# Transposing batch 3's last keys, queries and u with the DMA crossbar instead of TensorE

## The chip, the cores and the metric

The kernel runs on one core of a Trainium2 chip. Its engines are TensorE (PE, with its weight loads as PEld), VectorE (DVE), ScalarE (ACT), GpSimd (POOL) and SyncE (SP), which here only issues transfers; sixteen DMA engines carry these out. The metric is the device time of one execution in microseconds (us). Before the change it is 174.1 us, the median of 3 runs (174.01 to 174.3).

## The reference

Four batches, eight heads, 768 tokens, 48 columns a head. A recurrence with a decay per key column gives x (768 tokens by 384 columns in each batch), and a mixer over tokens and then channels follows:

```
state = alpha_t * state + k_t (outer) v_t        # per batch and head, 48 x 48
x_t   = q_t . state                              # heads side by side: x is 768 x 384
h  = relu(x^T @ w_tok1) @ w_tok2                 # over tokens, 768 -> 256 -> 768
u  = x + h^T
out = u + relu(u @ w_ch1) @ w_ch2                # over channels, 384 -> 1536 -> 384
```

## The kernel before

**Tiling.** A batch is six chunks of 128 tokens; chunks are numbered through the batches, so batch 3 has 18 to 23. Inputs are float32, and all that TensorE reads is bf16. Batch 0 and parts of batch 1 take chunks in pairs (`paired_chunks`); the later ones go by `natural_run`, and only those matter here.

**A chunk.** ACT takes the logarithm of alpha (`la`). PE sums it over the tokens with a triangular matrix (`cum`, L352), ACT exponentiates with both signs (`ek`, `eq`), and GpSimd multiplies keys and queries with the results (`pkk`, `pkq`, L275), eight heads of 64 columns each, 48 of them used. `s_transpose` brings both into a layout with columns on the partitions: `row_tiles` (L289) has PE transpose 64 x 64 pieces through an identity, sixteen a chunk, into two banks, and `s_transposed` (L297) copies the two banks to `tkq` on ACT or DVE. Then PE multiplies keys with queries (`gt`, L387), DVE masks (`gm`, L309), and PE forms the output of the chunk (`y`, L423, with the state's share in `between`, L338). The state goes through `state` (PE, L411), `st` (DVE) and `ss` (GpSimd, L322); GpSimd also makes `al` and casts v (`vb`). The output is evicted as `x`.

**The mixer.** For a batch with all six x: `tok1` (L602), a relu (`ht`), `tok2` (L651), and `u`, which DVE adds into the x tiles (L657). The channel part needs u with the columns on the partitions. In batches 1 to 3 (`separate`) PE transposes three chunks at a time with `row_tiles` (`utp`, 18 pieces of 64 x 64 for each half of the batch), and ACT and DVE copy them to `ut` (L669). Batch 0 (`mixed`) computes u transposed directly. `channel` then has 24 `ch1` (L691, three matmuls of 384 columns each), their relu (`rt`, L589 and L591), and for each chunk `ch2` in three parts of four matmuls (L715), the sum `o` (L728) and the store.

**What sets the order.** One list, `ORDER`, written out in numbers. Each item is an operation of the graph in the order of its creation, with the engine (A, D, P) where there is a choice and the banks behind a point; `f` is a matmul on zeros (`fill`, L792) that keeps PE busy and computes nothing. Each engine takes its own operations in that order, and waits in it. ch1 and ch2 of one batch stand between the chunk work of the next. All transfers are issued by SP, in the same order too: 86 loads and 25 stores. The tiles of the chunks come round: four `pkk`, `pkq` and `tkq`, six `o`, twelve x, two `ut`.

Of the kernel before, what the change touches and what calls it, by code (L numbers as in the profile page):

```python
# [17 lines left out]
FUSE = 99  # L18
FETCH, BLOCK, AHEAD, ARRIVES = 193, 256, 449, (4.5, 30.0, 3.0)
# [6 lines left out]
0 1 f0 2 f0 f0 f0 f0 f0 3 f0 f0 f0 f0 f0 4 28 f0 29 f0 f0 30.0 5 31.1 32 f2 f2 38 6 f2 35 f2 33 f2 f2 f2 39 f2 34 f2  # L26
36 40 f2 43.2 41 7 f3 66 47.3 f4 65 48 44 49A 50D f4 67.4 46A 45D 68.5 69 f6 51.67 75 72 54.01 8 70 52 f3 f3 76 f3 73
f3 77 f3 80.3 78 f2 9 84.2 56 f6 85 105 81 71 f6 104 87D f6 f6 10 86A f6 f6 83D 106.6 82A 55 107.5 108 53 91.14 11 114
88.23 92 f0 42P 37A f0 f0 109 90 f0 58.07 115 89 57.13 60A 93 f2 116 12 f2 f2 59 f2 f2 f2 112 f2 111 63 61 117 14
123.2 64A f0 62 f0 124 74A 79P 119.0 110 16 120 125D 126A f4 94.41 122A 121D 18 96 127.57 97 130.36 95.20 128 113A  # L30
118P 100 132 98 102 133.4 99A 20 131 13P f5 103A 169.5 101 163.6 24 166.2 f3 15P 129 141.3 135 142.0 143 136 134.17
17P 137 139 145 138D 147 140A 144 146 259 148 150 149 151 19D 152 172.4 178.1 162A 161D 175.7 f0 173 176 174A 167 177D
260 164 168A 170 22D 21P 165A 179 f0 171A 23D f0 261 f0 180A f0 189.0 201.3 190A 195.4 262 202A 181.7 27D 25P 196A
185.2 26D 182A 153 193.6 186A 211.5 264 194D 223.1 263 212D 227.0 224A 265.3 228A 266.4 155 267 217.7 273 270 207.2
274 209.6 268 300 208D 218A 276 213.5 210D 215.1 214A 269 187.0 301 271 216A 203.4 188A 219.3 275 204A 302 225.2 220A
154D 199.7 272 226A 278.65 277 279 200A 303 221.1 280D 281A 156P 183.0 222A 282 283 184A 292.43 284D 285A 197.2 304
294 286.71 157 305 198D 289.05 205.6 287 306.4 288 206A 159 191.2 308 291 307.7 309 311 239.6 296 314 343 290 315
249.1 297 192D 293.54 344 312 319.37 298 295A 345 254.0 316 299A 234.2 158A 346 317 244.5 347 310 313 160D 240 318 348
245 351 241 349 320 352.4 242A 321D 246 322A 354 235 247D 353 350 358 236 356 243 323 362 324 237D 333.64 357 325A
326D 376.5 238 363.2 335 250 248 355 364 336 486 365 327.37 251 487 329 366 367 330.62 328 252A 488 255 332 368 256  # L40
339 369 359.73 331 257A 370.12 340 229.4 361A 360D 253 372D 371A 377 373.60 258 510 334.73 375 489 381.21 341 490 374
337 230 342A 378 382 338A 491 379.5 383 231 380A 492 384.0 232D 511.6 385A 493 513 388.3 512 516 233 386.2 389A 514
517 494 521 495 515 387D 522.7 390.1 496 523 398.5 391 524 394.4 526 396.0 399 392.6 395 400.3 527 535.2 393 518.17
401 497 402.54 528 519A 397 529.63 525 403A 553.1 404D 498 520A 536 405.05 530A 416.4 499 554 406A 440.7 407D 555 531A
500 417D 420.2 539 434.6 421D 441A 501 532.10 435A 550.53 534 422.4 502 430.2 551 546 423A 540.7 533 431A 452.6 558
552 442.0 541 537.5 453D 503 542 438.4 544 538D 559.2 439A 556.1 443D 504 560 543 412.3 545 557D 561 426.6 413D 505
432.7 564 427A 410.5 506 433A 446.4 562 411A 565 408.0 507 447A 563 572.1 577 450.2 409D 508 454.3 573 451A 547.67 574
455D 566.54 509 548A 578.0 549D 591.1 568A 567D 448.2 720 592 580 424.3 584 449D 579 588.76 583 721 425A 569.54 590
418.1 596 582 436.2 570 419A 414.0 571 437A 581 597.3 593 589 722 610.6 575.5 598 444.1 415D 599 601 723 576A 594.2
611 445A 481.4 595D 602 724 744 428.7 476.0 600 429A 725 603 604.35 612 585.61 605A 726 466.2 587D 586A 477 727 606A  # L50
482 728 607.73 751 615.16 609 483 729 755 616 471.5 608 478 617 613.3 730 479 472 614A 484 618.1 480 762 456.7 619D
473 485 773 622.6 731 474 732 620.0 623A 475 457 621A 733 458 734 634.3 459 630.4 735 628.1 635 632.5 631 624.6 780
460 626.0 629 461.7 625 792 736 627 462 737 633 463 636.34 738 464 639.16 637A 467 638D 640A 641D 465 468 799 774.0
469 745.5 775 793.7 656.4 746 778 747 756.3 470 650.6 795 739 757 749 684.1 651D 740 758 644.2 685D 776 748 662.5 794
760 645D 741 660.6 811 663D 657A 678.3 750 742 661D 787.0 769.1 679A 812.7 770 759 668.2 743 777 813 761 672.5 788 814
664.4 669A 673D 789 670.6 665A 666.3 779 671A 646.1 830 667D 682.0 798 647A 831.7 683A 806.2 781.54 797 832 807 763.63
833 752.10 765D 658.2 783A 835 754D 764A 674.7 753D 659D 782A 686.3 808 675D 800.40 687A 803.16 796 802D 816 784.25
801A 766.73 804 680.0 768 818 654.4 681A 836 767 648.1 655A 844.3 786 642.0 649A 817 771.7 785 822.41 643A 652.5 772A
805 834 837 790.2 824 815 653A 809.0 791A 823 838.76 810A 819.51 825.2 839D 820A 828.4 840D 676.0 821A 826 715.7 829D
827 677A 849.65 841.21 845 716 843 846 700.4 851 695.0 850 696 842 852.3 688.1 853D 847.5 689A 705.6 848D 697 854.2  # L60
698 699 717 855A 710.3 718 711 701 719 702 856.1 703 704 712 857A 690.5 713 858.0 714 868.2 859 862.7 860.4 869 864.1
863 866.3 691 861 867 692 865 706 693 873.02 694 870.74 874A 875D 707 871D 872A 910.3 708 894.1 911A 709 880.5 895A
908.2 881D 906.0 909A 912.7 907A 900.4 913A 876.6 901A 896.3 877A 918.1 897A 914.5 919D 904.2 915A 922.0 905D 902.7
923D 920.4 903A 898.6 921A 916.3 899A 888.1 917A 890.5 889A 884.2 891D 878.0 885A 886.7 879A 882.4 887A 892.6 883D
929.3 893A 939.1 930 931 940 932 944.5 933 945 946 934.2 947 941 948 924.0 942 925 943 926 935 927 936 928 949.7 937
950 938 951 954.4 955 952 956 953 957 958
# [12 lines left out]
class Graph:  # L79
# [5 lines left out]
    def add(self, name, costs, emit, reads=(), writes=(), prio=0, dma=None, new=(), tail=0.0, rows=False, loose=False, n=0, late=0.0):  # L85
        self.ops.append(Op(costs, emit, new))
        return self.ops[-1]
# [6 lines left out]
def kernel(  # L94
# [12 lines left out]
    nc = tc.nc  # L107
    B, H, S, D = q.shape
    C = 128
# [232 lines left out]
    def natural_front(n):  # L342
# [7 lines left out]
        def cum(e):  # L350
# [3 lines left out]
            for j in range(4):  # L354
                pe.matmul(ps[:, HD + j : HD + j + 1], lhsT=la[:, 2 * j : 2 * j + 2, :], rhs=ones_col,  # L355
                          start=True, stop=True, skip_group_check=True)
# [478 lines left out]
```

## Time and profile before

| what | value |
|---|---|
| median of 3 runs | 174.1 us |
| the profiled execution | 174.24 us |
| its span, first to last instruction | 172.5 us |
| PE busy | 166.5 us, 96% |
| DVE, ACT, POOL busy | 102.0, 96.0, 72.3 us |
| HBM read and written | 25.17 and 4.72 MB |

Times in the profile count from the start of the span. A row of the groups has the line, engine and operation, what it writes and reads, how many there are, then busy time and mean duration in nanoseconds, then idle time just before them and what ended it. The end of a matmul is modelled, and matmuls overlap, so PE's pace is better read from the chain of waits, where many of one kind stand in one stretch: 72 matmuls of 384 columns in 11.70 us. SPq is SP's own queue. Releasers are inferred.

### The profile page before, as it was taken

The page shows a single profiled execution, that of the slowest core. Times are in us where ns is not written, and L with a number is a line of the kernel's source. Part 1 is how long each engine was busy: PE and PEld are TensorE (multiplying, and loading weights), DVE is VectorE, ACT ScalarE, POOL GpSimd, SP SyncE. Part 2 cuts the span into 40 slices and gives each one's busy share as a digit, 9 for nine tenths or more (in the row PEclk, how much of TensorE's full clock was granted, in tenths as well). Part 3 has the DMA queues.
Part 4 walks back from the last instruction along what each step waited for, and adds up shares of the span by engine and source line. Part 5 has one row for each costly group of instructions (what it writes and reads, how often), then busy time and mean ns, then how long its engine had stood idle before and what let it go on. Part 6 is the DMA issues. An engine that isn't in the chain of part 4 may idle for free.

```text
span 172.5 us, 5143 instructions
## 1 busy us (share of the span) xinstructions
PE 166.5 (96%) x2099; PEld 106.8 (62%) x2099; DVE 102.0 (59%) x212; ACT 96.0 (56%) x206; POOL 72.3 (42%) x114
## 2 busy tenths in 40 slices
PE   7999979999999999999999999999999999999993
PEld 3566656665666567566666665666676656656562
DVE  3159977544653597689593727495988248132231
ACT  2577552699865655497887231699771112865000
POOL 7252542319485782944877111499941000000000
PEclk9999999999999999999999999999999999999999
DMA  5999999999998999999999999995000221100133
GB/s 134 261 261 265 232 335 398 309 234 337 256 307 168 205 254 219 225 170 198 165 204 151 196 219 223 211 210 92 4 4 0 79 104 50 46 4 0 46 115 113
DMA packets 86150, 30.20 MB, mean 175 GB/s; under 512 B 79600, under 2 KB 85104, under 8 KB 86128
## 3 DMA queue, kind: packets, MB, share of 16 engines
q1 hardware_dynamic: 86128, 29.89, 75.2%
q8 instruction: 16, 0.26, 0.7%
q14 instruction: 6, 0.05, 0.1%
HBM read 25.17 MB, written 4.72 MB: 173 GB/s over the span
## 4 chain that ended last, share of the span: by engine, by line
PE 78%; DVE 6%; POOL 4%; DMA 3%; issue 3%; ACT 2%; SPq 1%; DVEq 0%; POOLq 0%
PE bank L691 27%; PE bank L715 23%; PE bank L289 4%; PE bank L651 3%; DMA ina<-in_alpha_dram 3%; PE bank L602 3%; DVE gm L309 2%; PE bank L387 2%; PE bank L338 2%; PE bank L423 2%; POOL pkk L275 2%; PE bank L521 1%; PE bank L411 1%; PE bank L352 1%; SPq L205 1%
## 5 line engine op out<-in xcount | busy, mean ns | idle before, releaser
L691 PE MATMUL bank<-ut,wc 128*128 128x384 bf16 x288 | 51.1, 326 | 0.0
L691 PEld LDWEIGHTS <-wc 128*128 128x128 bf16 x288 | 26.6, 98 | 16.5
L275 POOL TENSOR_TENSOR pkk<-ink,ek 128x384 bf16<-128x384 f32 x24 | 24.3, 1022 | 17.7 <-ACT ek L256 14.9
L715 PE MATMUL bank<-wc,rt 128*128 128x384 bf16 x144 | 26.5, 326 | 0.0
L715 PE MATMUL bank<-wc,rt_late 128*128 128x384 bf16 (+2 forms) x156 | 25.1, 314 | 0.0
L728 DVE TENSOR_TENSOR o<-bank,x 128x384 f32<-128x384 f32 (+2 forms) x19 | 10.1, 536 | 18.2 <-PE bank L715 18.2
L589 ACT ACTIVATE rt<-bank 128x384 bf16<-128x384 f32 x33 | 16.3, 494 | 7.4 <-PE bank L691 7.0
L282 POOL CAST vb<-inv 128x384 bf16<-128x384 f32 x21 | 10.5, 506 | 22.3 <-DMA inv<-in_v_dram 17.6
L715 PEld LDWEIGHTS <-rt_late 128*128 128x128 bf16 x156 | 14.4, 98 | 8.2
L275 POOL TENSOR_TENSOR pkq<-inq,eq 128x384 bf16<-128x384 f32 x18 | 17.9, 1003 | 2.8 <-ACT eq L258 2.8
L589 ACT ACTIVATE rt_late<-bank 128x384 bf16<-128x384 f32 x33 | 16.1, 495 | 5.3 <-PE bank L691 5.3
L309 DVE TENSOR_TENSOR gm<-bank,u 128x512 bf16<-128x512 f32 x28 | 17.3, 682 | 2.8 <-PE bank L387 2.6
L243 ACT ACTIVATE la<-ina 128x384 bf16<-128x384 f32 x24 | 12.1, 526 | 10.8 <-DMA ina<-in_alpha_dram 10.8
L715 PEld LDWEIGHTS <-rt 128*128 128x128 bf16 x144 | 13.2, 98 | 7.7
L792 PE MATMUL bank<-zeros 128*128 128x384 bf16 x61 | 15.1, 372 | 1.4 <-DVE la L192 1.2
L591 DVE TENSOR_SCALAR rt_late<-bank 128x384 bf16<-128x384 f32 x15 | 8.3, 554 | 10.0 <-PE bank L691 8.3
L309 DVE TENSOR_TENSOR gm<-bank,pmask 128x512 bf16<-128x512 f32 x20 | 12.7, 682 | 1.4 <-PE bank L521 1.3
L256 ACT ACTIVATE ek<-bank 128x384 f32<-128x384 f32 x24 | 11.4, 498 | 3.5 <-PE bank L355 2.0
L333 ACT CAST x<-bank 128x384 bf16<-128x384 f32 x16 | 7.3, 483 | 10.6 <-PE bank L338 9.4
L322 POOL TENSOR_TENSOR ss<-st,al 128x384 bf16<-128x384 f32 x12 | 10.0, 832 | 7.4 <-DVE st L319 5.4
L591 DVE TENSOR_SCALAR rt<-bank 128x384 bf16<-128x384 f32 x15 | 7.9, 554 | 5.3 <-PE bank L691 5.3
L297 ACT COPY tkq<-bank 128x512 bf16<-128x512 bf16 x17 | 9.3, 602 | 2.8 <-PE bank L289 2.7
(118 smaller groups left out, 237.3 us busy)
## 6 DMA issues: line engine op xcount, KB each, us to landing
out_dram<-o SPq DMA_DIRECT2D x23, 192.0 KB, 2.6
ina<-in_alpha_dram SPq DMA_DIRECT2D x14, 192.0 KB, 4.3
ink<-in_k_dram SPq DMA_DIRECT2D x14, 192.0 KB, 4.6
inq<-in_q_dram SPq DMA_DIRECT2D x14, 192.0 KB, 4.5
inv<-in_v_dram SPq DMA_DIRECT2D x14, 192.0 KB, 4.4
rt_late<-in_moe_w_ch_dram SPq DMA_DIRECT2D x2, 1152.0 KB, 10.1
rt_late<-in_moe_w_ch_dram SPq DMA_DIRECT2D x4, 576.0 KB, 7.1
ina<-in_alpha_dram SPq DMA_DIRECT2D x5, 384.0 KB, 6.3
```

The lines of the kernel that those rows point to most:

```text
L243: g.add("la", {"ACT": 0.43}, lambda e: act.activation(la[:, :, 0:D], t, AF.Ln), key, [u["la"][1]], pr + 5)
L256: g.add("ek", {"ACT": 0.38}, lambda e: act.activation(ek, banks[bank.place][:, 0:HD], AF.Exp, scale=-1.0), [bank], [kek], pr + 4)
L275: lambda e, dst=dst, src=src, ex=ex: {"POOL": gps, "DVE": dve}[e].tensor_tensor(dst[:, :, 0:D], src, ex().rearrange("p (h d) -> p h d", h= ...
L282: lambda e: evict[e](vb, src), ksrc, [u["vb"][1]], pr + 4)
L309: g.add("gm", {"DVE": 0.60}, lambda e: dve.tensor_tensor(gm, banks[bank.place].rearrange("p (j t) -> p j t", j=4), wide(mask, [[0, 4], lis ...
L322: g.add("ss", {"POOL": 0.79}, lambda e: gps.tensor_tensor(ss, st.rearrange("p (h d) -> p h d", h=H), wide(al, [[1, 8], [0, D]]), ALU.mult) ...
L589: act.activation(dst, src, AF.Relu)
L591: dve.tensor_scalar_max(dst, src, 0.0)
L691: pe.matmul(banks[bank.place][:, 0:HD], lhsT=wc1[wp][:, kc, off : off + 128], rhs=ut_t[b % 2][:, kc, cs], start=(kc == 0), stop=(kc == NM ...
L715: pe.matmul(banks[bank.place][:, 0 : hi - lo], lhsT=rt_t[(b * NDC + mc) % NRT][:, i * 128 : i * 128 + 128], rhs=wc2[:, mc, lo:hi], start=( ...
L728: g.add("o", {"DVE": 0.09 + 0.38 * width}, lambda e, i=i, bank=bank, o=o, lo=lo, hi=hi: dve.tensor_tensor(o[:, lo:hi], banks[bank.place][: ...
L792: pe.matmul(banks[place][:, 0:HD], lhsT=zeros[:, 0:128], rhs=zeros, start=True, stop=True, skip_group_check=True)
```

## The change

Two transposes go from PE to the crossbar of the DMA engines, from SBUF to SBUF, issued by SP: keys and queries of chunks 21, 22 and 23 (`TRD`), one transfer of 128 x 512 each, so six; and u of batch 3 (`UTD`), one transfer of 128 x 1152 for each half, so two. PE's 84 pieces for them and the ten copies out of the banks go. For this the x tiles of three chunks are laid side by side, and `ut` has chunk, column block, token as its order instead of column block, token; ch1 reads three pieces of 128 columns. `TOT` (another part, about the sums) is off. Beside that `ORDER` is new from start to end, 63 fillers instead of 61, and the engines of some copies and casts differ: of the 14 weight casts ACT has 6 instead of 1, DVE 4 instead of 7, POOL 4 instead of 6.

```diff
+UTD, TRD, TOT = (3,), (21, 22, 23), False
@@ ORDER, its first line; the others read alike
-0 1 f0 2 f0 f0 f0 f0 f0 3 f0 f0 f0 f0 f0 4 28 f0 29 f0 f0 30.0 5 31.1 32 f2 f2 38 6 f2 35 f2 33 f2 f2 f2 39 f2 34 f2
+0 1 f0 2 f0 f0 f0 f0 f0 3 f0 f0 f0 f0 f0 4 29 f0 28 f0 f0 30.0 5 31.1 32 f2 f2 38 6 f2 35 f2 33 f2 f2 f2 39 f2 36 f2
...
-    x_t = many("x", NX, [128, HD])
+    x_all = many("x", 4, [128, 3, HD])
+    x_t = [x_all[n // 3][:, n % 3, :] for n in range(NX)]
...
-    ut_t = many("ut", 2, [128, NM, S])
+    ut_t = many("ut", 2, [128, NCH, NM, C])
...
     def s_transpose(n, dst, key, prio):
         u, tb = units[n], [Bank(), Bank()]
+        if n in TRD:
+            for i, w in enumerate("kq"):
+                src, ksrc = u["p" + w]
+                g.add("trd", {"SP": 1.2}, lambda e, i=i, src=src: nc.sync.dma_start_transpose(
+                    dst[:, i], src.rearrange("p h d -> p (h d)")), [ksrc], [(*key, i)], prio, dma=0.8)
+            return
         g.add("tr", {"PE": 0.25}, lambda e: row_tiles(tb, sources(n)), [u["pk"][1], u["pq"][1]], tb, prio, new=tb, rows=True)
         s_transposed(n, tb, dst, key, prio)
...
+            if b in UTD:
+                x = x_all[(n0 + mine[0]) % NX // 3]
+                g.add("utd", {"SP": 1.3}, lambda e, x=x, cs=cs: nc.sync.dma_start_transpose(
+                    ut[:, cs].rearrange("p i j t -> p (i j) t"), x.rearrange("p i d -> p (i d)")), ku,
+                    [("ut", b % 2, j, part, h) for j in range(NM) for h in range(2)], 1000 * b + 170, dma=1.6)
+                continue
...
-                              rhs=ut_t[b % 2][:, kc, cs], start=(kc == 0), stop=(kc == NM - 1),
+                              rhs=ut_t[b % 2][:, ti, kc, :], start=(kc == 0), stop=(kc == NM - 1),
```

The costs in the braces feed the search for the order, and nothing at run time. In the changed kernel the lines are some 6 to 21 further down: gt is L402, ch1 L712, ch2 L736, the u sum L672.

SP's program, before, from the last loads on (numbers behind a name tell buffers apart):

```order
L205 DMA ink_106<-in_k_dram 128x8x48
L205 DMA inq_110<-in_q_dram 128x8x48
L205 DMA inv_114<-in_v_dram 128x8x48
L731 DMA out_dram<-o_198 128x384
L731 DMA out_dram<-o_202 128x384
```

The same place now; tkq_148, tkq_149 and tkq_150 are chunks 21, 22 and 23, and x_168 and x_169 the halves of batch 3's u:

```order
L206 DMA inv_114<-in_v_dram 128x8x48
L308 DMA_TRANSPOSE tkq_148<-pkk_124 128x4x128
L308 DMA_TRANSPOSE tkq_148<-pkq_120 128x4x128
L308 DMA_TRANSPOSE tkq_149<-pkk_125 128x4x128
L308 DMA_TRANSPOSE tkq_149<-pkq_121 128x4x128
L308 DMA_TRANSPOSE tkq_150<-pkk_126 128x4x128
L308 DMA_TRANSPOSE tkq_150<-pkq_122 128x4x128
L752 DMA out_dram<-o_189 128x384
L752 DMA out_dram<-o_193 128x384
L682 DMA_TRANSPOSE ut_175<-x_168 128x9x128
L682 DMA_TRANSPOSE ut_175<-x_169 128x9x128
L752 DMA out_dram<-o_192 128x384
```

Eight transfers stand behind the last load; two stores of batch 2 come between the chunks' and u's, the other four behind.

DVE's program from the last mixer's u to the channel part, before (the x on both sides are the tiles that u is added into):

```order
L657 TENSOR_TENSOR x_176<-bank_64,x_176 128x384
L657 TENSOR_TENSOR x_175<-bank_62,x_175 128x384
L728 TENSOR_TENSOR o_197<-bank_66,x_166 128x384
L669 COPY ut_183<-bank_63 128x3x3x64
L669 COPY ut_183<-bank_68 128x3x3x64
L728 TENSOR_TENSOR o_200<-bank_67,x_169 128x384
L591 TENSOR_SCALAR rt_late<-bank_66 128x384
```

And now:

```order
L672 TENSOR_TENSOR x_169<-bank_61,x_169 128x384
L672 TENSOR_TENSOR x_169<-bank_64,x_169 128x384
L749 TENSOR_TENSOR o_192<-bank_66,x_167 128x384
L749 TENSOR_TENSOR o_194<-bank_68,x_167 128x384
L749 TENSOR_TENSOR o_190<-bank_62,x_166 128x384
L606 TENSOR_SCALAR rt_late<-bank_67 128x384
```

The two copies of ut are gone from DVE (the other two from ACT), and three sums of batch 2's output stand between u and the first relu instead of two: on PE eight parts of ch2 now lie between tok2 and the first ch1 of batch 3, where four and the transposes lay.

More of the change, by code (lines that the diff above doesn't have):

```diff
@@ L31 @@
[L31 to L35, printed above, removed]
@@ L67 @@
+928 936 929 923 930 938 931 939 919 940 924 941 920 942.2 921 925 943 944 926 947.6 948 945 949 946 950 951
 """
@@ L83, in __init__, with add @@
         self.ops = []
-    def add(self, name, costs, emit, reads=(), writes=(), prio=0, dma=None, new=(), tail=0.0, rows=False, loose=False, n=0, late=0.0):
+    def add(self, name, costs, emit, reads=(), writes=(), prio=0, dma=None, new=(), tail=0.0, rows=False, loose=False, n=0, late=0.0, banks=(), gates=()):
         self.ops.append(Op(costs, emit, new))
```

105 lines of the change are left out of this document (58 added, 47 removed).

## Prediction

> **What bounds the kernel now.** I read the page's head and slices first, to see which engine is full and when.
>
> ```profile
> span 172.5 us, 5143 instructions
> PE 166.5 (96%) x2099; PEld 106.8 (62%) x2099; DVE 102.0 (59%) x212; ACT 96.0 (56%) x206; POOL 72.3 (42%) x114
> PE   7999979999999999999999999999999999999993
> ACT  2577552699865655497887231699771112865000
> POOL 7252542319485782944877111499941000000000
> DMA  5999999999998999999999999995000221100133
> ```
>
> Each digit stands for 4.3 us. TensorE is full from its second slice to its last but one. The DMA engines are full until about 120 us and nearly idle afterwards; GpSimd is full from about 112 to 125 us, where batch 3's chunks are prepared. A full PE could still be a PE whose instructions stretch, so the waits of PE come second.
>
> ```profile
> PE bank L521 <- DVE tk L479: 1.4, 2, 1.0
> PE bank L792 <- DVE la L192: 1.2, 1, 1.2
> PE bank L651 <- DVE ht L591: 0.2, 1, 0.2
> ```
>
> (Total, times, longest.) These are all, and two of them belong to the start. After that PE waits for nothing worth naming. The chain of waits, read third, says the same in order of time (start, length, what):
>
> ```profile
> 33.09 4.39 PE bank L691 x27
> ...
> 109.98 0.16 PE bank L352
> ...
> 118.89 0.81 PE bank L289 x48
> ...
> 121.27 0.34 PE bank L289 x16
> ...
> 125.63 0.20 PE bank L423 x8
> 125.83 0.17 PE bank L338 x4
> ...
> 126.37 0.57 PE bank L289 x32
> ...
> 128.73 0.55 PE bank L387 x16
> ...
> 141.03 1.95 PE bank L651 x12
> 142.98 1.95 PE bank L715 x12
> 144.93 0.63 PE bank L289 x36
> ...
> 146.31 11.70 PE bank L691 x72
> 158.01 11.74 PE bank L715 x84
> 169.76 0.02 issue
> 169.78 0.29 DVE o L728
> ```
>
> So the end is the sum of PE's work from the first L691 (33.1 us) on: what PE need not do there comes off the end one for one, and a tile that reaches PE late goes on it one for one. The rest of the span, 2.7 us behind 169.78, is the last store, which the change leaves as it is.
>
> **What is removed.** L289 transposes in pieces of 64 x 64. The x48 of 118.89 are chunks 20, 19 and 18 (sixteen each), the x16 chunk 21, the x32 chunks 23 and 22, the x36 batch 3's u. Gone are x16, x32 and x36: 0.34 + 0.57 + 0.63 = 1.54 us. Chunk 20 now stands apart from 18 and 19, and a split group costs more: 0.57 (32 pieces) + 0.34 (16) instead of 0.81, that is 0.10 more. Net 1.44 us.
>
> Ten evictions go as well, six of 512 columns and four of 576:
>
> ```profile
> L297 DVE COPY tkq<-bank 128x512 bf16<-128x512 bf16 x11 | 4.2, 418 | 2.0 <-PE bank L289 1.8
> L669 ACT COPY ut<-bank 128x576 bf16<-128x576 bf16 x6 | 3.7, 649 | 7.4 <-PE bank L289 7.4
> ```
>
> That is 0.42 to 0.65 us each on DVE and ACT. I count nothing for them: PE's work covers them now, and ACT even stands 7.4 us before its ut copies.
>
> **What is added.** Two zero fillers (61 to 63), of 0.1625 us each at PE's pace for 384 columns (11.70 / 72): 0 to 0.33 us, depending on whether they stand in a wait that exists anyway. I take 0.15, since fillers precede instructions that wait. ch1 now reads ut as three pieces of 128 columns. The cumulative sum of L352 already reads its 384 columns as eight pieces of 48, at the same duration as ch1, so I take 0:
>
> ```profile
> L691 PE MATMUL bank<-ut,wc 128*128 128x384 bf16 x288 | 51.1, 326 | 0.0
> L352 PE MATMUL bank<-la,u 128*128 128x384 bf16 x14 | 4.5, 327 | 0.0
> ```
>
> **Where the new transfers stand.** They start on a queue that has nothing else left: all loads are issued ahead of them, and the DMA share is near 0 by then. Behind them on SP stand only stores; nobody waits for these before an o buffer comes round. So only PE's five new waits count: chunk 21, chunks 23 and 22, the halves of u. For each I set when the source is ready against when PE arrives.
>
> PE's position follows from counting the orders. Up to batch 3's first cum the new order has the same PE work less one part of ch2 (four matmuls, 1.95 / 3 = 0.65) and plus the fillers: 109.98 - 0.65 = 109.3. From there to chunk 23's gt the old order took 128.73 - 109.98 = 18.75; the new one has one ch1 (0.49) and two ch2 (1.30) more, one y (0.20 + 0.17) and 0.81 of transposes less: 19.4, so 128.7. From there to tok2: old 12.3, new six ch2 (3.90) and one ch1 (0.49) less, one y more: 8.3, so 137.0. Six tok2 (1.95) and eight ch2 (5.20) then lead to the first ch1 at 144.1, and its fourth, the first to read the second half, at 145.6. Chunk 21's gt comes at about 125.
>
> GpSimd makes the sources:
>
> ```profile
> 110.89 1.96 POOL L275 TENSOR_TENSOR pkk<-ink,ek 128x384 bf16<-128x384 f32 x2 [0.27 <-ACT ek L256]
> 112.81 0.21 POOL L265 TENSOR_TENSOR al<-eq,bm 128x8 f32<-128x8 f32 x1
> 116.29 0.83 POOL L322 TENSOR_TENSOR ss<-st,al 128x384 bf16<-128x384 f32 x1
> 122.80 0.50 POOL L282 CAST vb<-inv 128x384 bf16<-128x384 f32 x1
> ```
>
> Its first pkk follows the first cum by 0.9 (109.98 to 110.89; sum and ek lie between): 110.2 in the new order. Until chunk 23's pkq is done it has twelve products (0.98 each), six al, two vb and one ss: 11.8 + 1.2 + 1.0 + 0.8 = 14.8, so 125.0, and **3.7 us** are left before PE needs it at 128.7. Chunk 21's pkq ends after eight products, four al and one ss, 119.7, and has 5.3 us.
>
> ```profile
> 141.39 2.88 DVE L657 TENSOR_TENSOR x<-bank,x 128x384 bf16<-128x384 f32 x6 [0.42 <-PE bank L651]
> ```
>
> DVE's six u begin 0.36 after tok2 does and take 2.88. With tok2 at 137.0 the third is done at 138.8 and the sixth at 140.2. The two halves have **5.3 and 5.4 us**.
>
> **The price of a transposing transfer** is in no row. One moves 128 KB (chunk) or 288 KB (half of u). The bounds are the transfers that there are (KB each, us to landing), and the time that SP takes to issue one:
>
> ```profile
> out_dram<-o SPq DMA_DIRECT2D x23, 192.0 KB, 2.6
> inq<-in_q_dram SPq DMA_DIRECT2D x14, 192.0 KB, 4.5
> ink<-in_k_dram SPq DMA_DIRECT2D x5, 384.0 KB, 7.7
> out_dram<-o SPq DMA_DIRECT2D x1, 128.0 KB, 1.7
> out_dram<-o SPq DMA_DIRECT2D x1, 64.0 KB, 1.5
> 114.32 0.73 SPq L205 DMA_DIRECT2D inq<-in_q_dram  x1
> ```
>
> Low end, stores on idle engines: 0.73 + 1.7 = 2.4 for a chunk (3.7 are there), and 0.73 + 2.6 x 288/192 = 4.6 for half of u (5.3 are there). No stall. High end, the loads among full engines: 0.73 + 4.5 puts chunk 23 at 130.2, 1.5 late; 0.73 + 7.7 puts the first half at 147.2 against 144.1, 3.1 more; the second half then comes in time. 4.6 us of stall in all. I take the low end, because the engines are as idle there as under the late stores. No gain beyond the 1.44 can come from the transfers, since PE alone sets the end.
>
> **Sum.** The profiled execution took 174.24 us with a span of 172.5, 0.14 above the median of 174.1. 174.24 - 1.44 + 0.15 = 172.95; less the 0.14, **172.8 us**, 0.75% faster, with 172.2 to 173.5 as its own range: the fillers' 0.33, and some tenths either way for an order that was made anew from start to end.
>
> **The rivals.** *A, the chunk stage is set by GpSimd after all.* POOL's 9s from 112 to 125 speak for it: what PE drops among the chunks (0.81) would turn into waiting for products, and only the u transposes (0.63) come off: 174.1 - 0.63 + 0.15 = 173.6. Against it stands PE without a wait in that stretch, with batch 2's ch1 between.
>
> *B, the tiles come late.* PE waits at chunk 23's gt, at the first ch1, or both. It begins where a product-to-landing time passes 3.7 us or a u-to-landing time passes 5.3, and costs each microsecond beyond. For it: a half of u has under 1 us of reserve even at the low end, and two halves share the engines. Half of the high end, 2.3 us, gives 175.1; all of it 177.4. Slower than before.
>
> *C, the change does not do what it says:* the order's other moves open a wait that eats the gain. In the new order ACT takes two of the token weights' casts before the first ch1 and one of ch1's just behind it, which DVE and GpSimd had. A 1152-column cast on ACT is this long, so a 768-column one is about 0.77:
>
> ```profile
> L762 ACT CAST wc<-rt_late 128x1152 bf16<-128x1152 f32 x1 | 1.2, 1152 | 0.4 <-DMA rt_late<-in_moe_w_ch_dram 0.4
> ```
>
> Two of them in the way of ACT's evictions cost some 1.3 us of start: 174.1. Against it: ACT is half busy there (the fifth to seventh digit, 17 to 30 us, are 5, 5 and 2).
>
> *D, block by block.* The crossbar takes the 128 x 128 blocks one after another, each at a price of its own. By the nearest row, the 64 KB store, 1.5 us a block: the six chunk transfers (24 blocks, from 118.7) end at 154.7, 26 late; the halves of u then come 8 and another 12 late: 172.8 + 46, about 219. Nothing in this trace speaks for it but that no trace of it exists. [...]
>
> **How the numbers follow.** Forecast 0.45, A 0.12, B 0.25, C 0.12, D 0.06. A measurement of this kernel can tell about 0.2% (0.35 us) from no change: faster means under 173.75. Forecast and A are faster; of B I put 0.04 there, 0.05 at no change, 0.16 slower; of C 0.03, 0.05, 0.04; D is slower. Faster 0.64, same 0.10, slower 0.26. The range is 171.9 (a start that happens to lose fillers from the path) to 175.6 (B somewhat beyond its half): it leaves out D, the upper end of B and a little below.
>
> **What would show it.** Right: L289 has 48 pieces behind 105 us instead of 132; PE's waits name no tkq or ut; the first L712 of batch 3 (ch1) comes near 144.1 and the last matmul ends near 168.5; issue to landing of the chunk transfers is below 3.7 us and of the u transfers below 5.3. A shows as waits of PE for pkk, pkq or gm; B as PE waiting for a DMA at L402 or L712; C as a first ch1 later than 33.5; D as landings of five microseconds and more for a chunk, growing from one to the next. Wrong above all if the transposing transfer costs SP or the DMA engines much more than the stores and loads here do.

## The result, and the profile after

The changed kernel takes **172.94 us** in the median of four runs (172.61 to 173.09), the kernel before 174.12 beside it (174.01 to 174.3). The ratio is 0.9926, with an interval of 0.9908 to 0.9944. The forecast was 172.8. Two of the profiled runs of the experiments below, that of u by PE and that of chunk 20 too, were slow ones, over 1.5% above the fastest of their kernel, with batch 3 starting 2 us late; the ratios leave such runs out.

The head of the page and its slices, of the changed kernel:

```profile
span 171.4 us, 4991 instructions
PE 165.1 (96%) x2017; PEld 105.2 (61%) x2017; DVE 98.4 (57%) x204; ACT 97.6 (57%) x205; POOL 70.6 (41%) x113
PE   7889999999999999999999999999999999999993
DMA  5999999999997999989999999999640138001034
```

PE is as full as before and has 1.4 us less to do (165.1 for 166.5). In the DMA row two small humps have grown: the `64` behind 120 us are the chunks' transfers, where it was silent before, and the `138` around 140 us those of u, with two of batch 2's stores ahead of them. The waits of PE (total, times, longest) are these, all of them:

```profile
PE bank L813 <- DVE la L193: 1.2, 1, 1.2
PE bank L459 <- ACT la L244: 0.6, 1, 0.6
PE bank L536 <- DVE tk L494: 0.5, 1, 0.5
PE bank L536 <- ACT tq L496: 0.3, 1, 0.3
PE bank L290 <- POOL pkk L276: 0.3, 1, 0.3
```

None names `tkq` or `ut`: no transposed tile came late. The chain of waits of the changed kernel (start, length, what), where it answers the one shown of before:

```profile
32.87 1.13 PE bank L712 x7
...
108.13 1.41 PE bank L736 x8
...
114.99 0.57 PE bank L290 x32
...
121.48 0.34 PE bank L290 x16
...
128.98 0.55 PE bank L402 x16
...
137.26 1.95 PE bank L666 x12
139.21 5.20 PE bank L736 x32
144.41 10.72 PE bank L712 x66
...
168.60 0.29 DVE o L749
```

Of L290 only 48 pieces are left behind the first cum of batch 3, where 132 were: chunks 18 and 19 at 114.99 and chunk 20 at 121.48. (The prediction said behind 105 us; batch 2's 36 pieces at 107.5 still stand there, in both kernels.) The last sum, which follows the last matmul, starts at 168.60 instead of 169.78. How close the new transfers came is in SP's timeline (start, time in which SP is held, line, what) and in the time from issue to landing, for the chunks over all six transfers and then by the median of each group:

```profile
118.63 1.30 SPq L308 DMA_TRANSPOSE tkq<-pkk  x1
120.03 1.20 SPq L308 DMA_TRANSPOSE tkq<-pkq  x1
121.40 2.23 SPq L308 DMA_TRANSPOSE tkq<-pkk  x1
...
126.35 1.21 SPq L308 DMA_TRANSPOSE tkq<-pkq  x1
139.28 2.74 SPq L682 DMA_TRANSPOSE ut<-x  x2
```

```profile
DMA to landing us min/median/max: 2.4/2.5/4.1
...
tkq<-pkq SPq DMA_TRANSPOSE x3, 2.4
ut<-x SPq DMA_TRANSPOSE x2, 3.3
```

SP goes from one chunk transfer to the next with hardly a pause from 120 us on: 1.2 us each, and 2.23 for the third. The cause of that one is open: the last load, issued at 116.19, had landed 4.4 us later, before the third was issued. The second transfer, chunk 21's queries, is the one that took 4.1 us to land, until 124.2, still 1.0 before its gt at 125.19. The last was ready when POOL had made chunk 23's queries, at 124.6 (`pkq`, started at 123.61, 0.99 long), but was issued only at 126.35. It lands at 126.35 + 2.4 = 128.75, and PE takes it at 128.98: **0.2 us** are left in this execution. The halves of u, issued at 139.28 and 140.7, land at 142.6 and 144.0 for the ch1 at 144.41 and 145.9, with 1.8 us and more left.

### The profile page after: what moved, and what is told of

Its sections match the earlier page's. It is cut to its first block, busy times and chain, and to the rows that moved or that the text cites. A ratio compares the mean times of both kernels' runs of the same rounds, so it can differ in the third digit from the quotient of the medians.

```text
span 171.4 us, 4991 instructions
## 1 busy us (share of the span) xinstructions
PE 165.1 (96%) x2017; PEld 105.2 (61%) x2017; DVE 98.4 (57%) x204; ACT 97.6 (57%) x205; POOL 70.6 (41%) x113
## 4 chain that ended last, share of the span: by engine, by line
PE 80%; DMA 7%; POOL 3%; DVE 3%; issue 2%; ACT 2%; SPq 1%; DVEq 0%; POOLq 0%
PE bank L736 27%; PE bank L712 23%; DMA ina<-in_alpha_dram 4%; PE bank L813 3%; DMA rt_late<-in_moe_w_ch_dram 3%; PE bank L290 3%; PE bank L666 2%; PE bank L617 2%; PE bank L402 2%; PE bank L345 2%; PE bank L536 2%; POOL pkq L276 2%; PE bank L438 1%; POOL pkk L276 1%; SPq L206 1%
## 5 line engine op out<-in xcount | busy, mean ns | idle before, releaser
L712 PE MATMUL bank<-ut,wc 128*128 128x384 bf16 x288 | 51.6, 326 | 0.0
L712 PEld LDWEIGHTS <-wc 128*128 128x128 bf16 x288 | 26.6, 98 | 16.2
L736 PE MATMUL bank<-wc,rt 128*128 128x384 bf16 x144 | 26.6, 326 | 0.0
L736 PE MATMUL bank<-wc,rt_late 128*128 128x384 bf16 (+2 forms) x156 | 25.2, 314 | 0.0
L604 ACT ACTIVATE rt_late<-bank 128x384 bf16<-128x384 f32 x30 | 14.6, 492 | 16.5 <-PE bank L712 16.4
L736 PEld LDWEIGHTS <-rt_late 128*128 128x128 bf16 x156 | 14.5, 98 | 8.3
L736 PEld LDWEIGHTS <-rt 128*128 128x128 bf16 x144 | 13.2, 98 | 7.8 <-issue 0.2
L604 ACT ACTIVATE rt<-bank 128x384 bf16<-128x384 f32 x33 | 15.8, 491 | 3.2 <-PE bank L712 2.9
L606 DVE TENSOR_SCALAR rt_late<-bank 128x384 bf16<-128x384 f32 x18 | 9.5, 555 | 8.8 <-PE bank L712 8.6
L340 ACT CAST x<-bank 128x384 bf16<-128x384 f32 x18 | 8.4, 482 | 10.3 <-PE bank L345 6.2
L813 PEld LDWEIGHTS <-zeros 128*128 128x128 bf16 x63 | 6.2, 106 | 5.2 <-issue 1.7
```

Source lines behind the costliest of these rows:

```text
L604: act.activation(dst, src, AF.Relu)
L606: dve.tensor_scalar_max(dst, src, 0.0)
L712: pe.matmul(banks[bank.place][:, 0:HD], lhsT=wc1[wp][:, kc, off : off + 128], rhs=ut_t[b % 2][:, ti, kc, :], start=(kc == 0), stop=(kc == ...
L736: pe.matmul(banks[bank.place][:, 0 : hi - lo], lhsT=rt_t[(b * NDC + mc) % NRT][:, i * 128 : i * 128 + 128], rhs=wc2[:, mc, lo:hi], start=( ...
L813: pe.matmul(banks[place][:, 0:HD], lhsT=zeros[:, 0:128], rhs=zeros, start=True, stop=True, skip_group_check=True)
```

## The experiments

Theory: the gain is the matmul work taken off PE, and it comes off the end one for one, because the new order puts enough other PE work between the making of a tile and its use. The rivals were that the new order gains by itself, that the transfers' number or SP decides, and that a transposing transfer is cheap or dear whatever runs beside it.

On the chips of these runs the kernel before has medians of 174.4 to 174.75, and the first cum of batch 3 (L359, L352 before) starts anywhere from 108.75 to 111.82 us, as the loads come in. Beside each ratio to the runs of before on the same chip I therefore use a **stretch** of the profile: from the start of that first cum to the start of the last o sum. It is 169.78 - 109.82 = 59.96 us before and 168.60 - 109.37 = 59.23 in the changed kernel. (The first cum is taken from the timeline, which has the start of this matmul some 0.16 ahead of the chain's in each run.) Here are all of them:

| kernel | first cum | last o | stretch | median, us | ratio to before, interval |
|---|---|---|---|---|---|
| before | 109.82 | 169.78 | 59.96 | 174.12 | 1 |
| changed | 109.37 | 168.60 | 59.23 | 172.94 | 0.9926 (0.9908 to 0.9944) |
| changed, again | 109.34 | 168.57 | 59.23 | 173.26 | 0.9932 (0.9898 to 0.9966) |
| u by PE | 111.63 | 171.59 | 59.96 | 174.43 | 0.9966 (0.9934 to 0.9998) |
| chunks 21, 22 by PE | 109.57 | 169.80 | 60.23 | 174.04 | 0.9960 (0.9934 to 0.9986) |
| order of before, slipped | 110.76 | 175.59 | 64.83 | 180.13 | 1.0233 (1.0124 to 1.0341) |
| order of before | 110.43 | 173.97 | 63.54 | 180.09 | 1.0296 (1.0209 to 1.0382) |
| chunk 20 too | 111.82 | 173.04 | 61.22 | 175.61 | 1.0050 (1.0014 to 1.0086) |
| two spare transfers | 109.58 | 170.71 | 61.13 | 176.86 | 1.0092 (1.0052 to 1.0132) |
| batch 2's u too | 108.75 | 173.66 | 64.91 | 178.87 | 1.0237 (1.0205 to 1.0269) |
| fewer fillers | 109.98 | 169.21 | 59.23 | 174.24 | 0.9958 (0.9925 to 0.9990) |
| merged, chunk 20 too | 110.13 | 169.33 | 59.20 | 172.85 | 0.9924 (0.9883 to 0.9965) |
| the same again | 109.45 | 168.39 | 58.94 | 172.75 | 0.9900 (0.9866 to 0.9933) |
| merged, chunks 21 to 23 | 109.72 | 168.95 | 59.23 | 173.59 | 0.9953 (0.9925 to 0.9980) |

**The changed kernel again**, as the measure for the others.

```diff
(no edit)
```

> The changed kernel itself once more, beside the others of this group. All theories: 0.993 of before, 172.9 us where before takes 174.1; no PE wait for tkq or ut.

Its stretch is 59.23 to the hundredth, and again no wait of PE names a transposed tile. What differs in time lies ahead of batch 3. The third transfer and the last one of this execution:

```profile
121.40 1.52 SPq L308 DMA_TRANSPOSE tkq<-pkk  x1
...
125.64 1.21 SPq L308 DMA_TRANSPOSE tkq<-pkq  x1
```

Here the third holds SP for 1.52 us instead of 2.23, so the last one is issued 0.7 earlier and lands at 125.64 + 2.4 = 128.04, against a gt at 128.96: **0.9 us** are left. So the reserve is 0.2 to 0.9 us, by how long that one transfer is held.

**u goes back to PE.**

```diff
-UTD, TRD, TOT = (3,), (21, 22, 23), False
+UTD, TRD, TOT = (), (21, 22, 23), False
@@ ORDER, u's transposes and copies, behind the fifth part of ch2 after tok2
+867.06 870.35 868A 869D 871D 872A
```

> Batch 3's u goes back to PE and its four copies to ACT and DVE, behind five of the eight ch2 parts after tok2; all else as in the changed kernel. Theory (PE's work is the time): the 36 pieces cost their 0.63 us again, 172.9 + 0.6 = 173.5, with L290 having 84 pieces behind 105 us. Rival (the new order is the gain, the crossbar only moves work that was hidden): 172.9 as before. Rival (the u transfers held PE up unseen): below 172.9.

The chain of this kernel has the pieces on the path again:

```profile
144.72 0.63 PE bank L291 x36
145.35 2.06 PE bank L737 x12
```

The stretch grows from 59.23 to 59.96, 0.73 against 0.63 for the pieces. The 0.1 beyond them stands right behind: the twelve matmuls of ch2 that follow the pieces take 2.06 us, where twelve take 1.95 elsewhere in the chain. By the stretch the gain of u's part of the change is shown, and that it was on the path; by the runs alone it isn't, since 0.9966 (0.9934 to 0.9998) still touches the interval of the changed kernel.

**Chunks 21 and 22 go back to PE.**

```diff
-UTD, TRD, TOT = (3,), (21, 22, 23), False
+UTD, TRD, TOT = (3,), (23,), False
@@ ORDER: chunk 21's transposes beside chunk 20's, chunk 22's as a group of its own
```

> Chunks 21 and 22 go back to PE (21 beside chunk 20's pieces, 22 in a group of its own) with four copies; chunk 23 and u stay on the crossbar. Theory: 32 pieces return, 0.57 - 0.34 = 0.23 for the sixteen in a group that is there already and 0.34 for the group of its own, 173.5; the transfer of chunk 23's queries is then issued when the product is done (about 124.6) instead of 126.35, since four issues of 1.2 us ahead of it are gone. Rival (order is the gain): 172.9.

The stretch grows by 1.00, where 0.57 was expected. The chain shows most of the rest as no matmul work at all:

```profile
121.68 0.39 PE bank L291 x16
122.08 0.46 issue
122.53 0.59 ACT tkq L299
...
123.64 0.57 DVE st L327
```

The chain leaves PE there: it runs over the copies of the pieces out of the banks (`tkq`, on ACT) and the state update (`st`, until 124.21) before PE goes on. So the prediction's zero for evictions holds only where the order has room for them, and this order was made without them. With four transfers fewer ahead of it, chunk 23's last one was issued at 124.83 instead of 126.35, which shows that it is SP's queue that delays it. A transfer can also be held without a queue: u's two hold SP for 3.87 us here instead of 2.74, and land after 4.5 and 4.6, with the last load landed some 20 us before.

**The crossbar in the order of before.** Two kernels: in the first, by a slip in where the transfers stand, chunk 19's output is made with chunk 23's queries; the second has them right.

```diff
@@ ORDER: that of before; the "tr", "tp" and "ut" entries give way to the transfers in their places
-... 0 1 f0 2 f0 f0 f0 f0 f0 3 f0 f0 f0 f0 f0 4 29 f0 28 ...
+... 0 1 f0 2 f0 f0 f0 f0 f0 3 f0 f0 f0 f0 f0 4 28 f0 29 ...
```

> The order of before with the crossbar put in its places: each chunk transfer right behind the product that it reads, u's right behind the last sum it needs, PE's transposes and the ten copies out, nothing else moved. Theory: PE's 1.44 us go, but only four ch2 parts (2.6 us) stand between tok2 and the first ch1, which reads the second half first: sixth sum 3.2 us after tok2 begins plus 3.3 of landing against 4.6, so about 2 us of PE waiting for the u transfer, and up to 1 us more at the gt of chunk 22, whose queries go last: 174.1 - 1.4 + 2 to 3 = 174.7 to 175.7, slower than before. Rival (the crossbar alone is the gain, the order is incidental): 172.7.

> The order of before with the crossbar in its places, now with chunk 23's transfers behind chunk 19's output, which still reads the same tkq tile (in the run before this one they stood ahead of it, so chunk 19's output was made with chunk 23's queries, a part of the result that was changed there). Theory: PE has 1.44 us less to do, but the tkq tile comes free only near 125.5, SP needs 1.2 us for each of four issues by then, and the last lands near 130 against a gt at 127.8: about 2 us of PE waiting; and u's second half comes about 2.2 us after the first ch1 asks for it (2.5 us were measured in the run before): 174.1 - 1.4 + 2.2 + 2.2 = 177. Rival (the crossbar is the gain whatever the order): 172.7.

The first took 180.13 us, the second 180.09; 174.7 to 175.7 and 177 were expected. The waits of PE in the second from 110 us on:

```profile
PE bank L712 <- DMA ut<-x: 2.5, 1, 2.5
PE bank L402 <- DMA tkq<-pkq: 1.1, 1, 1.1
PE bank L402 <- ACT x L340: 0.8, 1, 0.8
PE bank L426 <- ACT x L340: 0.2, 1, 0.2
```

The same transfers, the same work taken off PE, and 3% slower instead of 0.7% faster. Take the 1.54 of the pieces (nothing is split here) from before's stretch, 59.96 - 1.54 = 58.42; the four waits, 4.6, bring it to 63.0, and 63.54 was measured; the 0.5 between is not placed. The profiled run took 178.69 us with a granted clock of 1.00. The other three of this kernel took 179.77 to 181.28 at a mean clock of 0.988 to 0.990, so some 0.8% of the 3% goes with the clock, on which more at batch 2's u. Between tok2 and the first ch1 this order has four parts of ch2 (2.6 us), the new one eight (5.2); a transfer of 3.3 us fits into the second alone. So the order is half of the change: without it the crossbar loses. What the new order would do without any crossbar was not run. With u or two chunks back on PE it loses what the pieces cost, or more: both together, an estimate, make 59.23 + 0.73 + 1.00 = 60.96, more than the 59.96 of before, so nothing here speaks for a gain by the order alone in this stretch.

**Chunk 20 by the crossbar too**, two more single transfers ahead of the six.

```diff
-UTD, TRD, TOT = (3,), (21, 22, 23), False
+UTD, TRD, TOT = (3,), (20, 21, 22, 23), False
```

> Chunk 20 goes to the crossbar too, ahead of the other six; its PE group (0.34 us) and two copies go. Theory: eight issues of 1.2 us from 117.6, when the last load is issued, end at about 127.2; the last lands near 128.4 to 129.4 against a gt of chunk 23 that comes at 128.6: 172.6 if it is in time, up to 0.8 us of PE waiting at the gt if the issues stretch as one did (2.2 us): 172.6 to 173.4. Rival (the transfers cost nothing however many): 172.6 with no wait.

```profile
120.56 1.62 SPq L308 DMA_TRANSPOSE tkq<-pkk  x1
...
130.81 1.21 SPq L308 DMA_TRANSPOSE tkq<-pkq  x1
```

```profile
PE bank L402 <- DMA tkq<-pkq: 2.0, 2, 1.6
```

These are the first and the last of eight issues and what PE waits for. The last one lands at 130.81 + 2.4 = 133.2, and PE stands at that gt 1.65 us. PE has 0.34 less to do, and the stretch is 1.99 longer. The median of 175.61 lies 2 us above the 172.6 to 173.4 that were expected. In this profile the loads came some 2 us late (first cum at 111.82), so the queue also began 2 us later than in the changed kernel; PE began as late, though. That rival B (the tiles come late) is one step away is shown; how much of the 1.99 comes from the two extra transfers alone is not.

**Two spare transfers**, which put that step alone into the changed kernel: chunk 23's keys go through the crossbar twice more, into tiles that nobody reads, ahead of the real two.

```diff
+    spares = many("spare", 2, [128, 4, 128])
...
+                    if (n, i) == (23, 0):
+                        for spare in spares:
+                            nc.sync.dma_start_transpose(spare, src.rearrange("p h d -> p (h d)"))
```

> The changed kernel with two spare transfers (chunk 23's keys into tiles that nobody reads) ahead of chunk 23's own. Theory: SP needs 1.2 us for each, nothing else is behind it, so the last chunk transfer is issued at 128.8 instead of 126.35 and lands 2.4 later, at 131.2, where PE asks at 129.0; the reserve of the changed kernel is 0.2 us, so 2.2 us of PE waiting at the gt of chunk 23 and 172.9 + 2.2 = 175.1. Rival (SP's time per transfer is covered, there is more reserve than that): 172.9 to 174.

```profile
124.54 2.52 SPq L312 DMA_TRANSPOSE spare<-pkk  x2
...
128.47 1.21 SPq L313 DMA_TRANSPOSE tkq<-pkq  x1
```

```profile
PE bank L408 <- DMA tkq<-pkq: 1.8, 1, 1.8
```

The two spares hold SP for 2.5 us, 2.6 with the pauses between issues, and PE waits 1.8 us. The stretch grows by 1.90. The 0.8 that the wait falls short of 2.6 agrees with the reserve of 0.9 that the changed kernel had when it was taken again, with its third transfer held 1.52 us; here it is held 1.53. What goes beyond the reserve costs the path in full, 1.3 us for each further transfer. The runs cost more than this profile: the profiled run took 175.21, near the 175.1 expected, but the median is 176.86, 3.6 above the changed kernel's 173.26 on the same chip, and seven of the ten have a mean granted clock of 0.99. None of those was profiled.

**Batch 2's u too**, two transfers amid the loads of chunks 22 and 23.

```diff
-UTD, TRD, TOT = (3,), (21, 22, 23), False
+UTD, TRD, TOT = (2, 3), (21, 22, 23), False
@@ ORDER, batch 2
-636.62 484 639.45 637A 462 638D 470 641A 640D 463
+636 637 483 469 734 484 462 470 463
```

> Batch 2's u goes through the crossbar as well, two transfers in the middle of the load stream, everything else as in the changed kernel. PE loses another 36 pieces (0.63 us by the row of batch 3's u). Theory (the transfers are cheap only because batch 3's stretch has idle DMA engines): among the loads a transfer needs 4.5 to 7.7 us to land, as loads do; batch 2's u is done at about 106 to 107 and its ch1 stands at about 110, so PE waits for ut 0.5 to 4 us, and SP, held 1.2 to 2.7 us, issues chunk 22's and 23's loads that much later: 173 to 176 us, a wait of PE for DMA ut at the first ch1 of batch 2. Rival (a transposing transfer costs the same whatever runs beside it): landings of 3.3 us, no wait, 172.9 - 0.6 = 172.3.

```profile
PE bank L712 <- DMA ut<-x: 4.1, 1, 4.1
```

```profile
108.36 4.08 SPq L682 DMA_TRANSPOSE ut<-x  x2
```

```profile
111.12 3.30 DMA ut<-x
114.46 3.04 PE bank L712 x9
```

u itself was done at 107.0. SP came to the first transfer at 108.36 and was held 4.08 us by the two (2.67 for the first, 1.32 for the second), against 2.74 on idle engines; the second was issued at 111.12 and landed 3.30 later, no slower than in silence. The landings of the four u transfers lie between 3.3 and 4.6. So of my theory, that a transfer beside the loads lands as late as a load does, only the first one's 1.3 us more is left, and landings of 4.5 and 4.6 came without loads too, at u in the run with two chunks on PE. What made the tile late was SP's queue, together with too little PE work to cover it. The median of 178.87 lies above the 173 to 176 expected, because the wait had a second price. The windows around its end (PE's granted clock is the number ahead of the DMA share):

```profile
113.00:114.00 1.00, 0.00 (x0) 0.00 (x0) 0.00 (x0) 0.00 (x0) 1.00 (x3) 0.97 1.00 181
114.00:115.00 1.00, 0.54 (x2) 0.25 (x2) 0.00 (x0) 0.00 (x0) 0.94 (x1) 0.50 0.91 181
...
117.00:118.00 1.00, 1.00 (x10) 0.63 (x9) 0.60 (x2) 0.00 (x0) 0.00 (x0) 0.82 1.08 295
```

At about 114.0, some 3.6 us after PE fell idle (110.35), the granted clock drops to half, and stays there for some 3.4 microseconds, as the shares 0.97 and 0.82 of the first and the last window place it: nine ch1 matmuls take 3.04 us instead of 1.46. 59.23 + 4.11 + 1.58 = 64.92, and 64.91 was measured.

A shorter wait did the same. In the profile of the slipped order PE waited 2.48 us for u, from 147.79 to 150.27, and the clock fell when it had just begun again:

```profile
150.00:151.00 1.00, 0.73 (x4) 0.46 (x5) 0.00 (x0) 0.00 (x0) 0.00 (x0) 0.84 0.67 247
151.00:152.00 1.00, 1.00 (x5) 0.46 (x3) 0.00 (x0) 0.49 (x1) 0.00 (x0) 0.50 0.06 16
...
154.00:155.00 1.00, 1.00 (x7) 0.62 (x6) 0.00 (x0) 0.85 (x2) 0.00 (x0) 0.95 0.00 0
```

Its 72 ch1 took 13.56 us instead of 11.70. In the second kernel's profile the same wait of 2.5 us left the clock at 1.00, and so did the 1.8 us behind the two spares. But 3.4 us at half make 1% of such a run (an estimate, 0.5 x 3.4 / 175), and a mean clock of 0.99 is what three of the four runs of the second kernel and seven of the ten with two spares show. How long PE waited in those is not known. From what length on a wait brings the clock down is not shown by these four profiles.

**Fewer fillers**: the eight between the first tok1 and the first ch1 go.

```diff
@@ ORDER, between the first tok1 and the first ch1
-140D f0 f0 149 ... 172.5 f2 f2 f2 173 ... 261 f2 f2 168A 171D f2 195.2
+140D 149 ... 172.5 173 ... 261 168A 171D 195.2
```

> The eight zero fillers between the first tok1 and the first ch1 are left out, the order else that of the changed kernel. Theory: fillers stand in waits that exist anyway (for loads and casts at the start), so PE arrives at the waits earlier and waits longer: 172.9 to 172.6, the first ch1 at the same place within 0.3 us. Rival (the fillers lie on the path, 0.16 each): first ch1 and end 1.3 us earlier, 171.6.

```profile
PE bank L712 <- DVE wc L777: 0.8, 1, 0.8
```

PE now has a wait for a weight cast that the changed kernel doesn't show; its first ch1 is where it was (32.92 for 32.87), the first cum of batch 3 at 109.98, not earlier but 0.6 later. The fillers stood in waits that exist anyway, as the theory had it, and they cost the path nothing. The runs, at 0.9958, don't get below the changed kernel's 0.9926, as the expectation of 172.6 to 172.9 had it; whether these fillers even gain something isn't shown.

**Keys and queries in one transfer.** If SP's issue is what is short, then a transfer of eight blocks should hold SP no longer than one of four. The two tiles of a chunk become one, and one transfer moves both; chunk 20 goes with them.

```diff
-UTD, TRD, TOT = (3,), (21, 22, 23), False
+UTD, TRD, TOT = (3,), (20, 21, 22, 23), False
...
-    pkq_t = many("pkq", NPK, [128, H, 64])
-    pkk_t = many("pkk", NPK, [128, H, 64])
+    pk_t = many("pk", NPK, [128, 2, H, 64])
+    pkk_t, pkq_t = [t[:, 0] for t in pk_t], [t[:, 1] for t in pk_t]
...
-                g.add("trd", {"SP": 1.2}, lambda e, i=i, src=src: nc.sync.dma_start_transpose(
-                    dst[:, i], src.rearrange("p h d -> p (h d)")), [ksrc], [(*key, i)], prio, dma=0.8)
+                g.add("trd", {"SP": 1.2}, lambda e, i=i: i and nc.sync.dma_start_transpose(
+                    dst.rearrange("p w j t -> p (w j) t"), pk_t[n % NPK].rearrange("p w h d -> p (w h d)")),
+                    [ksrc], [(*key, i)], prio, dma=0.8)
```

> Keys and queries of a chunk in one tile and moved by one transfer of eight blocks, four of them, chunk 20 included (its 0.34 us on PE go). Theory: SP's 1.2 us are per transfer and not per block (nine blocks of u took 1.25 to 1.35), so an issue still takes about 1.25; a landing about 3.1 (four blocks 2.4, nine 3.3). Chunk 23's then lands near 127.8 against a gt at 128.6: 172.6 us, no PE wait at the gt, 0.8 us of reserve. Rival (time goes by the block): an issue takes 2.4, landing near 5, and PE waits 1 us or more: 173.5 and more.

> The same as e8_merged_20, taken again beside the others on one chip: one transposing transfer of eight blocks for keys and queries of each of the chunks 20 to 23. Theory (SP's issue is per transfer and is what filled up with chunk 20 by single transfers): ratio below that of the changed kernel by 0.1 to 0.3%, that is 0.990 to 0.992. Rival (merging only brings chunk 20 back to where the changed kernel is): 0.993 as the changed kernel.

Then the merging alone, with chunk 20 on PE as in the changed kernel:

```diff
 UTD, TRD, TOT = (3,), (21, 22, 23), False
(the rest as above)
```

> The changed kernel with the keys and queries of a chunk in one tile and one transposing transfer of eight blocks for each of the chunks 21 to 23; chunk 20 stays with PE, the order of the other instructions is that of the changed kernel. Theory: PE does the same work as in the changed kernel (from the first cum of batch 3 to the last o 59.2 us by the matmul starts), so the time is the changed kernel's, ratio 0.993, and only the reserve grows: SP holds the last chunk transfer 1.2 to 1.6 us and issues it as soon as chunk 23's queries are there, at about 125.0 instead of 126.35. What the merged kernel with chunk 20 gains beyond it (59.2 to 58.9) is then PE's 0.34 for chunk 20's sixteen pieces. Rival: the transfers' number itself costs the path something, and merging alone gives 58.9 and 0.991. A third: eight blocks need 4 us to land, the last one comes after its gt at 129.0 and PE waits up to 0.5 us.

SP's transposing transfers for chunks (min/median/max ns in which SP is held, and the landings), first of the kernel with chunk 20, taken the second time, then of the merging alone:

```profile
L308 SPq DMA_TRANSPOSE tkq<-pk x4: 1234/1573/2059, 118.3 to 124.7; - x4
...
DMA to landing us min/median/max: 3.1/4.1/5.4
```

```profile
L308 SPq DMA_TRANSPOSE tkq<-pk x3: 1233/1332/1376, 119.9 to 125.0; - x3
...
DMA to landing us min/median/max: 3.1/3.3/4.2
```

With the loads over (the merging alone), eight blocks hold SP for 1.23 to 1.38 us, where four in the changed kernel mostly take 1.2 to 1.3: here the price of an issue is per transfer. The last transfer is now issued at 125.0, as soon as chunk 23's queries are there, lands after 3.1 us at 128.1, and PE comes for the tile at 129.3 (first cum 0.35 later than in the changed kernel). The reserve, 0.2 and 0.9 in the changed kernel, is now 1.2 us. And the stretch of the merging alone is 59.23, the changed kernel's: where nothing was late, being earlier gains nothing. With chunk 20 as well it is 58.94, 0.29 less for 0.34 of pieces removed; in the first of the two profiles PE waited 0.26 for a `vb` of POOL's and it was 59.20. So the step from four crossbar chunks being slower (61.22) to being faster (58.94) comes from halving SP's issues: with the four merged ones SP is through in 7.7 us, from 118.3 to 126.0, with the eight single ones in 11.5, from 120.6 to 132.0.

The kernel with four merged chunks has the lowest medians of all, 172.85 and 172.75, at ratios of 0.9924 and 0.9900. Their intervals overlap with the changed kernel's (0.9926 and 0.9932), so by the runs alone it isn't shown to be faster than that; the stretch says 0.0 to 0.3 us.

## Why the prediction was right, step by step

**The bound.** PE alone set the end, and work taken off it came off one for one: shown by the stretch, which in the undisturbed kernels follows the pieces on PE within 0.1 us.

**The terms.** Within the stretch the prediction had -1.44 for the pieces and +0.65 for the part of ch2 that moved behind the first cum, -0.79; measured -0.73. Summed over the chain from the first cum on, the pieces make 2.35 us before and 0.91 now, which is the -1.44; the moved part of ch2 makes +0.56, and the other lines add some 0.15. Ahead of it, the prediction had -0.65 and +0.15 for the fillers (0 to 0.33); the chain of waits gives the first cum at 109.98 before and at 109.54 now (108.13 + 1.41), that is -0.65 + 0.21. Together -1.18 where -1.29 was forecast, and 1.16 in the two profiled executions' own times (174.24 and 173.08).

The 0.21 is not the fillers', though. All of them, 61 before and 63 now, stand ahead of the first ch1 (the last starts at 32.8 and 32.5), and that ch1 began 0.23 earlier (33.10 and 32.87). Windows from there to the first cum show what ate this and more: PE's idle time grew by 0.22 (0.39 to 0.61), and its busy time fell by 0.43 (76.49 to 76.06), where the part of ch2 alone is 0.65; what makes the 0.22 between them isn't shown. So the fillers cost nothing here, and that their 0.15 comes close to the 0.21 is luck. The first cum varies by more than that anyway: 109.37 and 109.34 in the two profiles of the changed kernel, 109.34 to 111.82 over all kernels that are the same up to there.

**The positions.** Forecast and measured: chunk 23's gt 128.7 and 128.98, tok2 137.0 and 137.26, the first ch1 144.1 and 144.41, the last matmul's end 168.5 and 168.5 (the last 72 start at 158.71 and take 9.79), chunk 23's queries on POOL 125.0 and 124.6.

**The zeros.** Three pieces of 128 columns as ch1's right side cost nothing:

```profile
L712 PE MATMUL bank<-ut,wc 128*128 128x384 bf16 x288 | 51.6, 326 | 0.0
```

Before it was 326 ns as well, and by the chain 66 of them take 10.72 us, 0.162 each as in the 72 of before. The evictions cost nothing here, and some 0.3 to 0.4 us in the experiment that put two chunks' back.

**The price of a transfer.** The low end was the right one in the median: 2.4 us for a chunk where 2.4 was taken, 3.3 for half of u where 4.6 was. One chunk transfer took 4.1, above the 3.7 that the prediction had named as the limit; it was chunk 21's, which had a wider window. But the parts of the price were mis-sized, and this is the weak step of the prediction. "0.73 issue" was a load's; SP is held 1.2 us by a transposing transfer. One alone would not notice; the six in a row took SP 8.9 us in one execution of the changed kernel (118.63 to 127.56) and 8.2 in the other (118.62 to 126.85), and this queue, not POOL, decided when the last one left. The prediction gave chunk 23 a window of 3.7 us for 2.4, 1.3 us of reserve; 0.2 us were left in one execution and 0.9 in the other. The sentence that the transfers "start on a queue that has nothing else left" overlooked that they queue behind each other, and the DMA engines were not idle for the first: it was issued at 118.63, and the last load landed at 120.6. That the last tile still came in time is luck, since the prediction had not added up this queue. Two spare transfers made rival B true, and by their 1.3 us each one more would have (an estimate against the 0.9).

**The rivals.** A (POOL becomes the bound): PE waits 0.3 us for POOL in all. B (the tiles come late): not here, but in four of the experiments and the slipped one, at up to 4.1 us a wait, and from the point at which SP's queue or PE's cover ran out, as the prediction's condition had it; its prices lacked the granted clock of 0.50 that two profiles show. C (the new order opens a wait by ACT's casts): the first ch1 is at 32.87, 0.2 earlier than before. D (block by block): four blocks land in 2.4 us, eight in 3.1 to 3.3, nine in 3.3; there are longer landings, up to 5.4 with eight blocks, but nothing grows from one to the next in the changed kernel, where the six take 2.5, 4.1, 3.5, 2.4, 2.4 and 2.4. A block more costs about 0.2 us, on top of some 1.6 for the transfer (an estimate from these landings, of transfers that nothing delayed), not the 1.5 that D took from the 64 KB store. Beside ordinary transfers of the changed kernel the landings are alike, 3.3 us for 288 KB, where a store of 192 KB takes 2.9 in the median; SP's time is not, 1.2 to 1.3 us for half of u and 0.4 for a store in the median.

## What to carry to other kernels

Moving transposes from a full TensorE to the DMA crossbar gained just the matmul time here (1.44 us of pieces), and only with an order that has other TensorE work to cover making, queueing and landing of the tile: without the new order the same transfers made this kernel 3% slower. For a row of transfers on one queue, add up the queue's time for each issue, and set the last one's landing against its reader; one transfer for two tiles held SP 1.23 to 1.38 us here, where the two single ones take 2.4. A wait on TensorE of a few microseconds can be paid twice, where the clock comes back at half: it was granted at 0.50 after 2.5 and 4.1 us in two profiles, and at 1.00 after 1.8 and 2.5 in two others.

## What the runs showed of the hardware that was not expected

- A transposing transfer holds SP for 1.2 to 1.4 us whether it has four, eight or nine blocks, where the last four loads ahead of it in the changed kernel take 0.4 to 1.4. Now and then one is held longer: the third of the row 1.5 to 2.2 in most runs, one of eight blocks 2.1, one for u 2.67 amid the loads, and one for u 2.48 with the last load landed 20 us before. So the loads alone don't explain it; the cause is open.
- With single transfers back to back the DMA engines stand still for part of each: in the changed kernel their share is 0.64 to 0.68 from 125 to 127 us, while it is 1.07 from 141 to 142, with both nine-block transfers under way. SP sets the pace of the single ones there, not the engines.
- A nine-block transfer lands in 3.3 us on idle engines and, once issued, also in 3.3 beside the load stream (the second of batch 2's); 4.6 at worst, with loads and without.
- The granted clock fell to 0.50 some 3.6 us after PE fell idle in a wait of 4.1 us, and 2.9 us after in one of 2.5 us, when PE was at work again; both times it came back some 3.4 us later. Another wait of 2.5 us and one of 1.8 left it at 1.00 in their profiles.
